# Attention with a window and sinks, then a gated two-layer product: w_out's rows dealt by four over the partitions, and half the masks of three units moved to TensorE

## The chip, the cores and the metric

The kernel runs on one core of a Trainium2 chip. Times are device microseconds of one execution; the median of three runs of the kernel before is 230.49 us (229.34 to 231.1). The profile is one execution more, which took 229.0 us; its span, from the first to the last instruction, is 227.2 us. The granted TensorE clock was 1.000 in it.

The engines are called PE (TensorE, matrix products), PEld (its loading of weights, the operand that stays in the array), ACT (ScalarE), DVE (VectorE), POOL (GpSimd) and SP (SyncE, which here only issues transfers). On TensorE the result is written to PSUM banks, from which ACT and DVE read.

## The reference

```python
def _attn_ref(q, k, v, n_sink, window):          # q, k, v: (4, 8, 768, 64)
    scores = (1 / sqrt(64)) * q @ k.T
    rel = pos[:, None] - pos[None, :]
    keep = (pos[None, :] < 4) | ((rel >= 0) & (rel < 128))
    a = softmax(where(keep, scores, -1e9))
    return a @ v

def _moe_ref(x, w_in, w_out, beta):              # (3072, 512), (512, 2048), (2048, 512), (2048,)
    h = x @ w_in
    g = h * (1 / (1 + exp(-beta * h)))
    return g @ w_out                             # (3072, 512), float32
```

The attention's output, turned to (token, head and dimension), is `x`. Each of the 2048 hidden columns has its own beta, and each is also one row of w_out; so the hidden columns may be taken in any order, as long as w_in's columns, beta and w_out's rows are taken in the same one.

## The kernel before

**Tiles.** The 3072 tokens are cut into T = 0 to 7 of 384 tokens. A unit n = 0 to 31 is one pair of heads over one such tile; units 4T to 4T+3 make tile T. A hidden block i = 16 T + m is 128 hidden columns (m = 0 to 15) of tile T.

**A unit** has these steps: its q and k come in as rows and are transposed so that the head dimension lies on the partitions (by TensorE and a copy for units 0 to 11, `transpose_first` and `transpose_in`; by a transposing transfer later); TensorE makes scores, ACT takes their exponential into E, a mask of zeros and ones is multiplied onto E by DVE, or was added to the scores as a large negative number by TensorE (units 0 to 3, `add_mask`, a product with the identity that opens the accumulation); `attend` multiplies E with v and a column of ones (line 843, with the sinks at line 832); `normalise` takes the reciprocal of the sums (852) and multiplies (854); `transpose_out` turns the result into xT, by TensorE and a copy for units 0 to 7, by a transposing transfer on SP's queue (863) later. Units 4 to 7 go by `scores_by_banks` (789) and `mask_by_banks` (804): scores and masks come in two banks, one of 512 columns per head and one of 256.

**A hidden block** is four products of 384 columns with w_in as weights (887), ACT's tanh with `beta_half` as its scale (895), and DVE's `g` (908), which is h (1 + tanh(beta h / 2)). **The output** is a sum over 16 hidden blocks (m) for each 128 tokens: products of 512 columns with `g` as weights (922), called products below, into two accumulators `acc0` and `acc1`, then a copy and a transfer out.

**Order.** The program runs over steps s. From s = 0 to 15 come the hidden blocks of T = 0; then a gap of eight steps (GAP = 8), in which units 4 to 7 run and only products stand beside them; then all other hidden blocks, with the units of the next tile between. `products(s)` says how many products step s names. A planner (class `Prog`) then lists the instructions of each engine: it keeps a cost for each, picks at each point the instruction that can start first by its costs, and models transfers by a rate, a start-up time per queue (`QUEUE`) and a `TAIL`. Every engine carries out its list in that order. Where the planner sees TensorE idle for more than `IDLE` = 50 ns ahead of a next step it puts in fillers (914), products of ones that nothing reads, for the idle time and `MORE` = 60 ns on top.

**Transfers.** SP's queue loads q, k and v of units 0 to 3, then waits for w_in's second quarter and loads those of units 4 to 7, then waits for parts of w_out for those of units 8 to 11 (535, 544). POOL issues w_in (596, four loads), w_out (601, eight loads of two m each) and the later units' rows (570, 579). beta comes in on ACT's queue as 16 rows of 128 and is transposed by TensorE (968) and halved by DVE (970).

The lines that the change touches: `Prog` (112 to 118), `load_qk` (537), `load_w_out` (600), `scores_by_banks`, `mask_by_banks`, `hidden_matmul` (887), beta (945, 968), and the main program.

Of the kernel before, what the change touches and what calls it, by code (L numbers as in the profile page):

```python
# [11 lines left out]
DM, DF, NOUT = 512, 2048, 512  # L12
NTOK = B * S
# [33 lines left out]
PE_MASK = 4  # L47

# [23 lines left out]
def products(s):  # L72

    return 0 if s < NM else 3 if s < NM + GAP or s >= 2 * NM + GAP else 2 if s < NM + GAP + 2 else 1
# [23 lines left out]
class Prog:  # L98
# [14 lines left out]
    TAIL, MIX, HEAVY, RING = 900.0, 1.1, 2.5, 8  # L113
# [4 lines left out]
    IDLE, MORE, EARLY = 50.0, 60.0, 5500.0  # L118
# [251 lines left out]
def bass_streamingllm_window__then__act_swish_beta_kernel(  # L370
# [32 lines left out]
    beta_stage = sb("beta_stage", (16, 128), F32)  # L403
# [5 lines left out]
    ident32 = sb("ident32", (32, 32), F32)  # L409
    scratch = sb("scratch", (32, 1), F32)  # L410
    mask = [sb(f"mask{z}", (128, 6, 128), BF16) for z in range(2)]
    add_mask = sb("add_mask", (128, 6, 128), BF16)
    stage = {t: [sb(f"{t}_stage{z}", (128, 2, 6, D), F32) for z in range(4)] for t in "qk"}
# [178 lines left out]
    w_out_src = moe_w_out.rearrange("(m p) n -> p m n", p=128)  # L592
# [176 lines left out]
    def scores_by_banks(n):  # L769
# [3 lines left out]
        for bank, runs in enumerate(AT_ONCE[half]):  # L773
            of = 2 - 2 * bank
            names = HS_NAMES[of:of + 2]
            src = hs_ps[:, of:of + 2, :]
            with P.together("pe"):
# [7 lines left out]
                for kb, qb, nq in runs:  # L785
                    w = 128 * nq
                    for hh in range(2):
                        rows = slice(64 * hh, 64 * hh + 64)
                        op("pe", lambda e, at=at, w=w, kb=kb, qb=qb, nq=nq, hh=hh, rows=rows, of=of: e.matmul(  # L789
                            hs_ps[:, of + hh, at:at + w], keys_of(pb, rows, kb),  # L790
                            queries_of(pb, rows, qb, nq), start=True, stop=True),
# [7 lines left out]
    def mask_by_banks(n):  # L799
        z, half = n % NE, place(n)[2]  # L800
        for bank, cols in enumerate((slice(0, 512), slice(512, 768))):
            m = mask[half][:, :, :].rearrange("p m x -> p (m x)")[:, cols]
# [3 lines left out]
               r=[("E", z, bank), *MASK[half]], w=[("E", z, bank)], **dve(580.0 if bank == 0 else 290.0))  # L806
# [77 lines left out]
    def hidden_matmul(i, c):  # L884
# [3 lines left out]
            bank, w_in16[:, c, m * 128:(m + 1) * 128], xT[:, c, T * TT:(T + 1) * TT],  # L888
# [31 lines left out]
    def project(T, t, m, bank, name, eng="act", cols=slice(0, NOUT), queue="sp"):  # L920
# [24 lines left out]
    op("act", lambda e: e.dma_start(beta_stage[:, :], moe_beta.rearrange("(m p) -> m p", p=128)),  # L945
       w=["beta_stage"], dma="beta", busy=500.0, lag=100.0)
# [85 lines left out]
    for s in range(-2, S_END + NM):  # L1032
# [114 lines left out]
```

## Time and profile before

| | us |
|---|---|
| median of three runs (lowest, highest) | 230.49 (229.34, 231.1) |
| the profiled execution | 229.0 |
| its span | 227.2 |
| first hidden product (line 887) | 17.07 |
| first hidden product of T = 1 | 42.99 |
| first hidden product of T = 2 | 70.39 |
| last product with w_out begins at about | 224.2 |

The page's costliest groups for TensorE, with the number of instructions, their busy time and the mean duration of one (matmuls overlap, so their starts are closer than the duration):

| line, what | count | busy us | mean ns |
|---|---|---|---|
| 887, hidden blocks | 480 | 96.2 | 326 |
| 922, products with w_out | 340 | 93.8 | 380 |
| 843, attend | 348 | 17.3 | 193 |
| 914, fillers | 32 | 6.7 | 344 |

A row of the engine timeline reads: start in us, duration, engine, line, operation, what is written from what, shape, how many are merged in the row, and in brackets how long the engine had been idle before and what it had waited for. In the chain of waits each row is a start, a length and what the time went to.

### The profile page before, as it was taken

The page shows a single profiled execution, that of the slowest core. Times are in us where ns is not written, and L with a number is a line of the kernel's source. Part 1 is how long each engine was busy: PE and PEld are TensorE (multiplying, and loading weights), DVE is VectorE, ACT ScalarE, POOL GpSimd, SP SyncE. Part 2 cuts the span into 40 slices and gives each one's busy share as a digit, 9 for nine tenths or more (in the row PEclk, how much of TensorE's full clock was granted, in tenths as well). Part 3 has the DMA queues.
Part 4 walks back from the last instruction along what each step waited for, and adds up shares of the span by engine and source line. Part 5 has one row for each costly group of instructions (what it writes and reads, how often), then busy time and mean ns, then how long its engine had stood idle before and what let it go on. Part 6 is the DMA issues. An engine that isn't in the chain of part 4 may idle for free.

```text
span 227.2 us, 4402 instructions
## 1 busy us (share of the span) xinstructions
PE 218.2 (96%) x1721; PEld 122.1 (54%) x1749; DVE 133.0 (59%) x263; ACT 141.7 (62%) x210; POOL 125.4 (55%) x193
## 2 busy tenths in 40 slices
PE   7999978899999999999999999999999999999995
PEld 4665545454655555555555555555555555555454
DVE  4756878459974666666565656555666564443200
ACT  3778796259855777666657676666656755555310
POOL 6692387999996969995939398876300000000000
PEclk9999999999999999999999999999999999999999
DMA  5999989999999989999979999999911112110122
GB/s 168 255 191 215 280 194 151 204 242 206 123 148 177 159 89 151 123 161 134 120 110 157 98 134 139 121 154 138 140 24 52 52 26 64 46 49 0 60 79 95
DMA packets 98389, 29.70 MB, mean 131 GB/s; under 512 B 84912, under 2 KB 95424, under 8 KB 98368
## 3 DMA queue, kind: packets, MB, share of 16 engines
q0 software_dynamic: 55888, 10.52, 58.2%
q1 hardware_dynamic: 42304, 18.75, 36.5%
q8 instruction: 14, 0.23, 0.4%
q10 hardware_dynamic: 176, 0.14, 0.2%
q14 instruction: 7, 0.06, 0.1%
HBM read 27.32 MB, written 6.29 MB: 148 GB/s over the span
## 4 chain that ended last, share of the span: by engine, by line
PE 73%; DMA 14%; SPq 6%; DVE 3%; issue 2%; POOL 1%; ACT 0%; ACTq 0%
PE hs_ps L887 31%; PE acc L922 30%; DMA k_stage<-in_k_dram 4%; PE hs_ps L754 4%; SPq L535 4%; PE hs_ps L843 3%; DMA q_stage<-in_q_dram 3%; DMA w_in<-in_moe_w_in_dram 3%; SPq L544 2%; DMA w_out<-in_moe_w_out_dram 2%; DMA xT<-o_norm 2%; PE hs_ps L922 2%; POOL qk L650 1%; PE hs_ps L832 1%; DVE g L908 1%
## 5 line engine op out<-in xcount | busy, mean ns | idle before, releaser
L895 ACT ACTIVATE th<-hs_ps,beta_half 128x384 f32<-128x384 f32 x120 | 69.3, 582 | 61.8 <-PE hs_ps L887 61.1
L887 PE MATMUL hs_ps<-xT,w_in 128*128 128x384 bf16 x480 | 96.2, 326 | 0.6 <-issue 0.2
L922 PE MATMUL acc<-w_out,g 128*128 128x512 bf16 x340 | 93.8, 380 | 1.3 <-issue 0.5
L908 DVE SCALAR_TENSOR_TENSOR g<-th,hs_ps 128x384 bf16<-128x384 f32 x120 | 65.5, 550 | 42.8 <-ACT th L895 41.3
L887 PEld LDWEIGHTS hs_ps<-xT,w_in 128*128 128x128 bf16 x480 | 45.6, 98 | 38.5 <-DVE g L908 1.2
L922 PEld LDWEIGHTS acc<-w_out,g 128*128 128x128 bf16 x368 | 33.6, 98 | 30.2 <-issue 3.8
L570 POOL DMA_DIRECT2D land<-in_q_dram x40 | 30.6, 767 | 15.9 <-DVE rden L852 15.9
L766 ACT ACTIVATE E<-hs_ps 128x1920 bf16<-128x1920 f32 (+1 forms) x20 | 32.8, 1640 | 0.3
L811 DVE TENSOR_TENSOR E<-E,mask 128x1536 bf16<-128x1536 bf16 x20 | 19.2, 959 | 21.2 <-ACT E L766 21.2
L570 POOL DMA_DIRECT2D land<-in_k_dram x40 | 30.6, 767 | 0.0
L579 POOL DMA_DIRECT2D v_aug<-in_v_dram x40 | 30.6, 767 | 0.0
L930 ACT ACTIVATE out_sb<-acc 128x512 f32<-128x512 f32 x23 | 13.7, 597 | 7.3 <-PE acc L922 7.1
L843 PE MATMUL hs_ps<-v_aug,E 128*128 128x65 bf16 x348 | 17.3, 193 | 0.1
L843 PEld LDWEIGHTS hs_ps<-v_aug,E 128*128 128x128 bf16 x348 | 15.7, 97 | 2.7 <-issue 1.3
L854 DVE TENSOR_TENSOR o_norm<-hs_ps,rden 128x384 bf16<-128x384 f32 x29 | 16.1, 556 | 1.0
L727 ACT ACTIVATE E<-hs_ps 128x768 bf16<-128x768 f32 x16 | 12.6, 814 | 1.9 <-PE hs_ps L720 1.7
L832 PE MATMUL hs_ps<-v_sink,E 128*128 128x130 bf16 x48 | 9.3, 219 | 1.1 <-DVE E L804 1.1
L754 PE MATMUL hs_ps<-qkT 64*128 64x256 bf16 (+2 forms) x144 | 10.1, 254 | 0.0
L795 ACT ACTIVATE E<-hs_ps 128x1024 bf16<-128x1024 f32 x8 | 7.8, 1038 | 2.2 <-PE hs_ps L789 2.2
L650 POOL CAST qk<-k_stage 128x384 bf16<-128x384 f32 x12 | 6.3, 526 | 4.8 <-DMA k_stage<-in_k_dram 4.5
L852 DVE RECIPROCAL rden<-hs_ps 128x6 f32<-128x6 f32 x29 | 5.6, 193 | 3.8 <-PE hs_ps L843 3.7
L914 PE MATMUL acc<-ones 128*128 128x384 bf16 (+1 forms) x32 | 6.7, 344 | 1.2 <-DVE ones L457 1.2
(73 smaller groups left out, 148.1 us busy)
## 6 DMA issues: line engine op xcount, KB each, us to landing
out_dram<-out_sb SPq DMA_DIRECT2D x23, 256.0 KB, 2.7
q_stage<-in_q_dram SPq DMA_DIRECT2D x12, 192.0 KB, 6.4
k_stage<-in_k_dram SPq DMA_DIRECT2D x12, 192.0 KB, 6.2
w_in<-in_moe_w_in_dram POOLq DMA_DIRECT2D x4, 512.0 KB, 6.5
w_out<-in_moe_w_out_dram POOLq DMA_DIRECT2D x8, 256.0 KB, 5.9
land<-in_q_dram POOLq DMA_DIRECT2D x40, 48.0 KB, 3.7
land<-in_k_dram POOLq DMA_DIRECT2D x40, 48.0 KB, 3.6
v_aug<-in_v_dram POOLq DMA_DIRECT2D x40, 48.0 KB, 3.5
```

Of the source, the lines that this page charges most:

```text
L570: op("gp", lambda e, d=d, s=s: e.dma_start(d, s), w=[("land", pb, half, x, hh)], after=after, dma=f"l{pb}{half}{x}{hh}", **transfer(TT * D ...
L579: op("gp", lambda e, d=d, s=s: e.dma_start(d, s), w=[("v", pb, 3 * half + c, hh) for c in range(3)], after=after, dma=f"lv{pb}{half}{hh}", ...
L754: op("pe", lambda e, at=at, w=w, kb=kb, qb=qb, nq=nq, hh=hh, rows=rows, bank=bank: e.matmul(hs_ps[:, of + 2 * hh + bank, at:at + w], keys_ ...
L766: op("act", lambda e: e.activation(dst, src, AF.Exp, bias=0.0, scale=SCALE), x=list(names), w=[("E", z, 0), ("E", z, 1)], **act(1920 if ha ...
L811: op("dve", lambda e: e.tensor_tensor(E[z][:, :, 0:768], E[z][:, :, 0:768], m.unsqueeze(1).to_broadcast([128, 2, 768]), ALU.mult), r=[("E" ...
L843: last=(x == len(kbs) - 1): e.matmul(av_ps[:, at + hh * D1:at + hh * D1 + D1], E[z][:, hh, col:col + 128], v_aug[:, pb, hh, kb, 0:D1], sta ...
L854: op("dve", lambda e: e.tensor_tensor(o_norm[o][:, :, :, :].rearrange("p m h d -> p (m h) d"), src[:, :, 0:D], rden[z][:, :].unsqueeze(2). ...
L887: op("pe", lambda e: e.matmul(bank, w_in16[:, c, m * 128:(m + 1) * 128], xT[:, c, T * TT:(T + 1) * TT], start=(c == 0), stop=(c == 3)), r= ...
L895: op("act", lambda e: e.activation(th[i % 3][:, :], bank, AF.Tanh, bias=0.0, scale=beta_half[:, m:m + 1]), x=[name], r=["beta"], w=[("th", ...
L908: op("dve", lambda e: e.scalar_tensor_tensor(g[T % 2][:, m, :], th[i % 3][:, :], 1.0, bank, ALU.add, ALU.mult), r=[("th", i % 3)], x=[name ...
L922: op("pe", lambda e: e.matmul(bank[:, 0:width], g[T % 2][:, m, t * 128:(t + 1) * 128], w_out16[:, m, cols], start=(m == 0), stop=(m == NM ...
L930: op("act", lambda e: e.activation(out_sb[z][:, 0:width], bank[:, 0:width], AF.Copy, bias=0.0, scale=0.5), x=[name], w=[("out_sb", z)], ** ...
```

## The change

Four things are changed together.

1. Rows of w_out. Before, w_out's row m * 128 + p lay on partition p as block m. Now 512 rows at a time are dealt by four (`PER`): partition p holds rows 512 g + 4 p + j, j = 0 to 3, as blocks 4 g + j. A load of two blocks takes two neighbouring rows per partition as one piece of 4 KB (two pieces of 2 KB before). The hidden blocks take the same columns: the weights of block m are every fourth column of w_in from m % 4, within 512. beta is loaded straight into that order, by SP after the first loads of v, as 512 pieces of four numbers; ACT's load, its transpose on TensorE and the small identity for it are gone.
2. Masks. For the bank of 512 columns of units 5, 6 and 7 the mask is added by TensorE: a product of the identity with `add_mask1` (0 or -1e6) opens each head's accumulation, and DVE's multiplication for that bank is left out. `add_mask1` is made from the mask by one POOL instruction ahead of the first w_out load.
3. Products in the gap: steps 16 to 19 name none, steps 20 to 23 six each (three in each of the eight steps before).
4. The planner's numbers: `TAIL` 1100 (900), `MORE` 0 (60), DVE's mask costs 700 and 330 (580 and 290), w_out's rate 385 (350), and unit 8's q load counted 2300 ns late. Unit 7's copy of transposed q and k goes to DVE (ACT before).

The transfers, the products and the order that is planned change so:

```diff
+PE_MASK_BANKS = ((5, 0), (6, 0), (7, 0))
...
 def products(s):
 
+    if NM <= s < NM + GAP:
+        return (0,0,0,0,6,6,6,6)[s - NM]
...
-    TAIL, MIX, HEAVY, RING = 900.0, 1.1, 2.5, 8
+    TAIL, MIX, HEAVY, RING = 1100.0, 1.1, 2.5, 8
...
-    IDLE, MORE, EARLY = 50.0, 60.0, 5500.0
+    IDLE, MORE, EARLY = 50.0, 0.0, 5500.0
...
-           dma=f"{name}{pb}_{half}", seq="loads " + queue, late=3300.0 if (n, x) == (4, 0) else 0.0,
+           dma=f"{name}{pb}_{half}", seq="loads " + queue, late=3300.0 if (n, x) == (4, 0) else 2300.0 if (n, x) == (8, 0) else 0.0,
...
-    w_out_src = moe_w_out.rearrange("(m p) n -> p m n", p=128)
+    w_out_src = moe_w_out.rearrange("(g p j) n -> p g j n", p=128, j=PER)
...
-        op("gp", lambda e: e.dma_start(w_out16[:, m:m + ms, :], w_out_src[:, m:m + ms, :]), after=after,
+        op("gp", lambda e: e.dma_start(w_out16[:, m:m + ms, :].rearrange("p j n -> p (j n)"),
+                                         w_out_src[:, m // PER, m % PER:m % PER + ms, :].rearrange("p j n -> p (j n)")), after=after,
            w=[("w_out", mm) for mm in range(m, m + ms)],
-           dma=f"wo{m}", **transfer(ms * 128 * NOUT * 4, 350, 740.0, 3.0))
+           dma=f"wo{m}", **transfer(ms * 128 * NOUT * 4, 410 if ms == 4 else 385, 740.0, 3.0))
...
+            masked = (n, bank) in PE_MASK_BANKS
+            if masked:
+                cols = slice(0, 512) if bank == 0 else slice(512, 768)
+                with P.together("pe"):
+                    for x in range(2):
+                        op("pe", lambda e, x=x, of=of, cols=cols: e.matmul(
+                            hs_ps[:, of + x, 0:cols.stop - cols.start], ident[:, :], add_mask1[:, cols],
+                            start=True, stop=False, skip_group_check=True),
+                           r=["ident", "add_mask1"], w=[names[x]], **pe(cols.stop - cols.start))
...
         for bank, cols in enumerate((slice(0, 512), slice(512, 768))):
+            if (n, bank) in PE_MASK_BANKS:
+                continue
...
-               r=[("E", z, bank), *MASK[half]], w=[("E", z, bank)], **dve(580.0 if bank == 0 else 290.0))
+               r=[("E", z, bank), *MASK[half]], w=[("E", z, bank)], **dve(700.0 if bank == 0 else 330.0))
...
-            bank, w_in16[:, c, m * 128:(m + 1) * 128], xT[:, c, T * TT:(T + 1) * TT],
+            bank, w_in16[:, c, m // PER * 512 + m % PER:m // PER * 512 + 512:PER], xT[:, c, T * TT:(T + 1) * TT],
...
-    op("act", lambda e: e.dma_start(beta_stage[:, :], moe_beta.rearrange("(m p) -> m p", p=128)),
-       w=["beta_stage"], dma="beta", busy=500.0, lag=100.0)
...
+    op("sp", lambda e: e.dma_start(beta_raw[:, :].rearrange("p (g j) -> p g j", j=PER),
+                                   moe_beta.rearrange("(g p j) -> p g j", p=128, j=PER)),
+       w=["beta_raw"], dma="beta", seq="loads sp", busy=500.0, lag=300.0)
+    op("dve", lambda e: e.tensor_scalar(beta_half[:, :], beta_raw[:, :], 0.5, None, ALU.mult),
+       r=["beta_raw"], w=["beta"], **dve(100.0))
...
-    select(ident32[:, :], ones32[:, :], [[1, 32]], ALU.is_equal, 0.0, 0, -1, ["ones32"], ["ident32"])
     transpose_first(0)
-    op("pe", lambda e: nc.tensor.transpose(acc[1][:, 0:16], beta_stage[:, :], ident32[0:16, 0:16]),
-       r=["beta_stage", "ident32"], w=["acc1"], **pe(64))
-    op("dve", lambda e: e.tensor_scalar(beta_half[:, :], acc[1][:, 0:16], 0.5, None, ALU.mult),
-       x=["acc1"], w=["beta"], **dve(100.0))
...
+    op("gp", lambda e: e.tensor_scalar(
+        add_mask1[:, :], mask[1][:, :, :].rearrange("p m x -> p (m x)"), -1.0, -NEG, ALU.add, ALU.mult),
+       r=MASK[1], w=["add_mask1"], busy=1000.0, lag=140.0, after=[("v", 3, 0, 0)])
...
-                transpose_in(n, eng="act" if n in (5, 7) else "dve")
+                transpose_in(n, eng="act" if n in (5,) else "dve")
```

More of the change, by code (lines that the diff above doesn't have):

```diff
@@ L12 @@
 DM, DF, NOUT = 512, 2048, 512
+PER = 4
 NTOK = B * S
@@ L402, in bass_streamingllm_window__then__act_swish_beta_kernel @@
     w_out16 = sb("w_out16", (128, NM, NOUT), BF16)
-    beta_stage = sb("beta_stage", (16, 128), F32)
+    beta_raw = sb("beta_raw", (128, NM), F32)
     beta_half = sb("beta_half", (128, NM), F32)
@@ L408, in bass_streamingllm_window__then__act_swish_beta_kernel @@
     ones32 = sb("ones32", (32, 32), F32)
-    ident32 = sb("ident32", (32, 32), F32)
     scratch = sb("scratch", (32, 1), F32)
@@ L412, in bass_streamingllm_window__then__act_swish_beta_kernel @@
     add_mask = sb("add_mask", (128, 6, 128), BF16)
+    add_mask1 = sb("add_mask1", (128, 6 * 128), BF16)
     stage = {t: [sb(f"{t}_stage{z}", (128, 2, 6, D), F32) for z in range(4)] for t in "qk"}
@@ L788, in scores_by_banks @@
                         rows = slice(64 * hh, 64 * hh + 64)
-                        op("pe", lambda e, at=at, w=w, kb=kb, qb=qb, nq=nq, hh=hh, rows=rows, of=of: e.matmul(
+                        op("pe", lambda e, at=at, w=w, kb=kb, qb=qb, nq=nq, hh=hh, rows=rows, of=of, masked=masked: e.matmul(
                             hs_ps[:, of + hh, at:at + w], keys_of(pb, rows, kb),
-                            queries_of(pb, rows, qb, nq), start=True, stop=True),
+                            queries_of(pb, rows, qb, nq), start=not masked, stop=True,
+                            skip_group_check=masked),
                            r=keys_read(pb, half, runs), w=[names[hh]],
```

## The prediction

> **What bounds the kernel now.** First the page's busy times, then busy time by stage: T=0's attention (to 17.07 us), its hidden blocks (to 28.9), units 4 to 7 (to 43), T=1's hidden blocks (to 66.8), the rest.
>
> ```profile
> span 227.2 us, 4402 instructions
> PE 218.2 (96%) x1721; PEld 122.1 (54%) x1749; DVE 133.0 (59%) x263; ACT 141.7 (62%) x210; POOL 125.4 (55%) x193
> ```
> ```profile
> 17.07:28.90 11.83, 11.62 (x83) 6.89 (x80) 8.94 (x17) 9.73 (x20) 3.17 (x8) 1.00 1.20 250
> 28.90:43.00 14.10, 12.16 (x144) 6.86 (x146) 10.75 (x23) 9.36 (x11) 12.17 (x20) 1.00 0.99 171
> 43.00:66.80 23.80, 22.64 (x193) 12.10 (x194) 18.81 (x38) 15.73 (x26) 22.60 (x33) 1.00 1.62 187
> 90.90:150.00 59.10, 58.67 (x461) 32.44 (x468) 35.89 (x68) 38.65 (x55) 46.58 (x63) 1.00 1.23 132
> ```
> Columns: the stretch, its length, then busy PE, weight loads, DVE, ACT, POOL, granted clock, DMA share, GB/s. TensorE is the bound: from 90.9 to 150 it is idle for 0.4 us. Its idle time lies early: 1.94 us in units 4 to 7 (14.10 - 12.16), 1.16 in T=1's hidden blocks. A change that leaves the hidden blocks and products alone is worth that idle time plus what it moves ahead of 17.07, minus what it adds to PE. The PE timeline says what the largest idle pieces wait for:
>
> ```profile
> 33.26 0.23 PE L832 MATMUL hs_ps<-v_sink,E 128*128 128x130 bf16 x1 [0.76 <-DVE E L804]
> ...
> 35.82 0.23 PE L832 MATMUL hs_ps<-v_sink,E 128*128 128x130 bf16 x1 [0.32 <-DVE E L804]
> ...
> 45.48 0.34 PE L663 MATMUL hs_ps<-ident,qk 128*128 128x128 bf16 x3 [0.82 <-POOL qk L650]
> ```
> Two are waits for VectorE's mask, one for unit 8's cast, whose load waited for w_out: in the chain of waits w_out's landing (32.86 + 4.50) is followed by unit 8's q load (37.38 + 7.48) and this cast (44.92).
>
> **Masks on TensorE.** Removed from DVE: three masks of 128x1024, 0.68 us each (2.05). Added to PE: six matmuls of 512 columns; products of that width stand 0.216 us apart (three in 0.65), so 1.29 us. Unit 7's q/k copy goes from ACT (0.79) to DVE (0.94). Hidden in idle time the six cost nothing, and all 1.94 us filled would leave -0.65; on the path they cost +1.29. I replayed the new order by the rows' durations. Unit 5's pair (0.43) falls into the 0.76 that PE waits for unit 4's mask. That mask stays on DVE, and one of the 128x512 forms took 1.33 us where the shortest took 0.42, so unit 4's attend remains at about 33.3. Unit 6's pair follows that attend; unit 5's attend, relieved of its large mask, moves from 35.82 to about 35.5. Then what is late is unit 7's copy, now in DVE's queue ahead of unit 5's normalisation: the transposes out of unit 4 wait for its bank until about 36.4. The products held back for units 6 and 7 fill PE afterwards. T=1's first hidden block comes out at 42.9 (42.99 before), with 20 products done in both orders. I take 0.0, ends -0.65 and +1.29. The additive mask is built on POOL: 768 columns at the cast's 0.51 per 384, about 1.0 us, between 17.5 and the first w_out load at 18.11. It delays that load by 0.4; the load landed at 25.9 and its first product ran at 29.99: free. One new filler of 128 columns: +0.05.
>
> **w_out dealt.** Same bytes, eight loads of 0.716 us on POOL, half the pieces. The landings were 3.5 to 8.7 us; nothing waited on w_out but SP's loads of units 8 to 11 (8.4 us in three waits), and of these PE feels the 0.82 at 45.48. The new order also puts unit 8's q transposes after the third hidden block instead of the first, some 2 us later, so that idle goes with or without faster pieces: -0.82, at least 0.
>
> The price is in w_in: each hidden weight load now takes every fourth column, 8 bytes apart. No row shows that. The nearest are these:
>
> ```profile
> 12.51 0.55 PE L843 MATMUL acc<-v_aug,E 128*128 128x65 bf16 x12
> 12.89 0.32 PE L709 MATMUL hs_ps<-add_mask,ident 128*128 128x384 bf16 x1
> ```
> Twelve matmuls, each with its own load of 128 contiguous columns, took 12.89 - 12.51 = 0.38 us, 32 ns for a load and its matmul, although each load's record is 98 ns. A hidden block's matmul of 384 columns occupies PE for 162.5 ns (four in 0.65). Even at four times 32 ns, for four times the span of bytes, a strided load takes 127 ns and stays behind the matmul before it: 0. The other end, twice the 98 ns record with no overlap within it, is 196 ns: 512 x 33.5 = +17.2 us. A gain is excluded, since the loads are hidden already. The Trainium skill ("SBUF — State Buffer", in the section "Door 1") says that reads in the same 16-byte line run at full bandwidth if at least two fall in it. By it a step of 8 bytes costs nothing and the sum is the same; no run here shows it yet.
>
> **Beta.** Gone are ACT's issue (0.43), a POOL select (about 0.22) and a PE transpose at 3.30, while q and k of unit 0 were still on their way: 0. New is a load of 512 pieces of 16 bytes at the end of SP's first loads, and DVE's beta copy (0.17), which waits for it. Behind that copy in DVE's queue stands unit 1's reciprocal (13.09 before); for it wait accumulator 1, unit 2's attend and, through PE's order, the first hidden block. Nearest rows: the v loads issued just ahead on the same queue have 512 pieces each as well (of 256 bytes), were issued at 7.15 to 8.21 and landed 4.0 us later. The next issue is at 8.75, when SP has nothing to do until 17.84, where unit 4's loads wait for w_in, so its 0.5 of issue is free: landing at 12.75, copy done at 12.9, no wait. Ends: 2.1 us, beta's landing before; 7.9, the slowest v load, which lands it at 16.65 and moves the reciprocal by 3.7. I take 4.0. The pieces also cost the DMA engines 512 x 31.4 ns / 16 = 1.0 us (31.4 = 36.5% of 227.2 x 16 over 42304 packets), while w_in lands; its chunks have 1.4 us or more in hand (23.9 against 25.33 for the last), but unit 4's loads, which wait for the second, come up to 1.0 later and its k transposes stand only 0.65 later in the new order: 0 to +0.4, I take +0.2. The Trainium skill ("DMA: Bandwidth & Descriptors", Specifications) speaks against this edit: pieces below 512 bytes cost a read-modify-write. The v loads at 256 bytes lie below that line too, and landed in 4.0 us.
>
> **Fillers and order ahead of 17.07.** With 60 ns less per gap, seven fillers of 128 columns fewer run there. A filler of 0.22 us after unit 0's attend goes and unit 2's first scores move ahead of unit 3's k transposes: its exponential can start at 11.64 (11.91), unit 3's ends at 14.75 (15.2), the first hidden block starts at 16.65: -0.4. Unit 4's data don't come earlier, so I count -0.2, ends -0.4 and 0.
>
> **Into T=2.** PE now has 66 products done when it reaches T=2, 59 before, and unit 11's attend comes later. From its end to the fourth matmul of T=2, which reads unit 11's transposed output, stand 19 products (4.1), unit 12's scores (0.7) and three matmuls (0.5): 5.3 us. Before, the attend ended near 64.6, the normalisation at 65.78, and this row followed:
>
> ```profile
> 66.78 4.30 DMA xT<-o_norm
> ```
> That is 1.2 + 4.3 = 5.5 us without a queue, 1.0 more behind SP's transpose of unit 14, which stands ahead there in the new order too. PE waited 0.47 for it before. Change: -0.47 to +1.3; I take +0.2.
>
> **Sum.** 0.0 + 0.05 - 0.82 + 0 + 0.2 - 0.2 + 0.2 = -0.57, some -0.6: span 226.6, that execution 228.4 instead of 229.0 (1.8 around the span). The median of the three runs is 230.49, 1.5 above the profiled one; on it 229.9.
>
> **Rivals.** (1) PE's idle time goes altogether: -0.65 in units 4 to 7, -1.16 in T=1, -0.47 into T=2, -0.4 ahead of 17.07: -2.7, 227.8. For it: PE holds back products that can fill any gap, and DVE is relieved by 2.05 us. Against it: the wait for unit 4's mask stays, and the loads of unit 4 don't come earlier. Chance 0.32.
> (2) Beta lands late and DVE stands on it. At 7.9 us after issue the first hidden block starts some 3.5 later in place of 0.2 earlier, in all +3.1: 233.6. It decides from a landing 4.3 us after issue, and exceeds 1% from about 7. For: 512 tiny pieces in a saturated stage (DMA share 1.2). Against: the v rows. 0.12.
> (3) Strided weight loads come out from behind the matmuls, from 162.5 ns a load; at 196 ns +17.2 - 0.6: 247. Against: 32 ns a pair. 0.08.
> (4) Unit 11's output is the new wait into T=2, +1.3 instead of +0.2: 231.0. 0.08.
> (5) The change doesn't do what it says: w_out's landings stay and the 0.82 only moves to unit 8's or 9's later transposes: 230.7. 0.05.
>
> **Numbers.** Forecast 0.35. One per cent is 2.3 us and about what a measurement of this kernel can tell from no change. Faster by more: rival 1, 0.32. Within: 0.35 + 0.08 + 0.05 = 0.48. Slower: 0.12 + 0.08 = 0.20. Range 227.3 to 232.6: from just below rival 1 past rival 4 and the unfilled masks (229.9 + 1.29 = 231.2) into rival 2; rival 3 and the late end of rival 2 are left out.
>
> **What would show it.** Hidden matmuls still 0.65 us for four (else rival 3). DVE's beta copy starting before 13 and the first hidden block before 17.07 (else rival 2). Idle time of PE between 28.9 and 43 near 0.7, with a wait for unit 4's mask left, and T=1 starting near 42.9. No wait for unit 8's cast. A wait for unit 11's output below 0.7 us. The forecast is wrong if T=1's first hidden block moves by over 1 us, or if hidden blocks change their pace.

## The result, and the profile after

The kernel after takes 231.06 us (median of 14 runs, 229.53 to 233.5); the kernel before, run beside it, 229.93 (14 runs). The ratio is 1.0052, with a 95% interval of 1.0028 to 1.0077: slower by 1.2 us, within the one per cent that I called "same", but on the slower side of no change, where the forecast was on the faster. A ratio compares the faster executions of a kernel with those of before made beside it and leaves out the slower ones, so it need not be the quotient of the two medians. The profiled execution of after took 231.4 us, 2.4 more than that of before, so it shows the loss about twice as large as the runs do; single traces are read below for what waits on what, and the runs for what it is worth.

The page of after, its busy times:

```profile
span 229.7 us, 4436 instructions
PE 220.7 (96%) x1755; PEld 129.6 (56%) x1755; DVE 132.3 (58%) x261; ACT 141.8 (62%) x209; POOL 124.8 (54%) x193
```

Busy time by stage, in the stretches of the prediction (stretch, its length, busy PE, weight loads, DVE, ACT, POOL, clock, DMA share, GB/s):

```profile
17.07:28.90 11.83, 11.20 (x78) 7.39 (x77) 8.06 (x15) 9.21 (x19) 3.90 (x9) 1.00 1.13 226
28.90:43.00 14.10, 12.97 (x152) 7.27 (x151) 10.25 (x22) 9.62 (x11) 8.94 (x17) 1.00 0.87 154
43.00:66.80 23.80, 23.32 (x182) 12.90 (x181) 17.59 (x35) 15.03 (x24) 22.84 (x33) 1.00 1.60 204
90.90:150.00 59.10, 59.10 (x476) 35.04 (x475) 37.35 (x71) 40.24 (x57) 49.30 (x66) 1.00 1.29 133
```

TensorE is still the bound, with no idle time at all from 90.9 to 150. Where units 4 to 7 run it is idle for 1.13 us (1.94 before), DVE is busy for 0.5 us less, and the DMA engines moved 154 GB/s in place of 171. The trace of before needs care here: it has no record for 28 of the 368 products with w_out, though their weight loads are there. All of its 0.43 us of idle time from 90.9 to 150 stand at such products, and 0.37 of the 1.94. So 1.13 compares with about 1.6. The PE timeline says what it waits for now:

```profile
26.71 0.34 PE L669 MATMUL hs_ps<-ident,qk 128*128 128x128 bf16 x3 [0.46 <-POOL qk L656]
...
42.60 1.04 PE L940 MATMUL acc<-w_out,g 128*128 128x512 bf16 x4 [0.60 <-DMA w_out<-in_moe_w_out_dram]
...
44.06 0.39 PE L940 MATMUL acc<-w_out,g 128*128 128x512 bf16 x1 [0.42 <-DMA w_out<-in_moe_w_out_dram]
...
74.56 0.35 PE L905 MATMUL hs_ps<-xT,w_in 128*128 128x384 bf16 x1 [1.39 <-DMA xT<-o_norm]
```

Of the three waits of before, the two for VectorE's masks are gone (0.18 us for unit 5's second bank is left) and so is the one for unit 8's cast. Two new ones stand in their place: the products wait 1.02 us for w_out itself, which nothing on TensorE did before, and the fourth matmul of T = 2 waits 1.39 us for unit 11's output. (Before, TensorE had no idle time there: the weight load waited 0.47 us, and the matmul came 0.25 us behind its pace. In after the weight load waits 1.76, and the matmul comes 1.55 behind.) The first hidden block starts at 17.25 us (17.07), T = 1's at 45.10 (42.99), T = 2's at 72.52 with 66 products done (70.39 with 59).

How far one trace can be trusted shows in a kernel below that differs from before only in the stride of its weights and has a ratio of 1.0015: in its trace T = 1 starts at 44.36 and T = 2 at 72.54, both over 1 us later than in the trace of before. The trace of before is an early one of its order.

How late w_out lands is read from the tile's own view: the last four loads, and the time from issue to landing. Of before:

```profile
L601 POOL DMA_DIRECT2D w_out<-in_moe_w_out_dram x4: 716/716/716, 35.4 to 37.6; - x4
...
DMA to landing us min/median/max: 5.6/7.0/8.7
```

Of after:

```profile
L606 POOL DMA_DIRECT2D w_out<-in_moe_w_out_dram x4: 528/542/558, 36.5 to 38.1; - x4
...
DMA to landing us min/median/max: 7.5/8.9/10.5
```

POOL issues a load in 0.54 us in place of 0.72, and the three figures for the four loads are 1.8 to 1.9 us longer. So half the pieces didn't make the load faster.

### The profile page after: what moved, and what is told of

The parts are those of the page before. It is cut to its first block, busy times and chain, and to the rows that moved or that the text cites. A ratio compares the mean times of both kernels' runs of the same rounds, so it can differ in the third digit from the quotient of the medians.

```text
span 229.7 us, 4436 instructions
## 1 busy us (share of the span) xinstructions
PE 220.7 (96%) x1755; PEld 129.6 (56%) x1755; DVE 132.3 (58%) x261; ACT 141.8 (62%) x209; POOL 124.8 (54%) x193
## 3 DMA queue, kind: packets, MB, share of 16 engines
HBM read 27.32 MB, written 6.29 MB: 146 GB/s over the span
## 4 chain that ended last, share of the span: by engine, by line
PE 75%; DMA 7%; POOL 5%; issue 5%; DVE 3%; SPq 2%; ACT 2%; POOLq 0%; ACTq 0%
PE acc L940 31%; PE hs_ps L905 31%; PE hs_ps L760 4%; DMA w_out<-in_moe_w_out_dram 3%; PE hs_ps L861 3%; DMA xT<-o_norm 2%; SPq L540 2%; DMA k_stage<-in_k_dram 2%; PE hs_ps L940 2%; POOL qk L656 1%; DVE g L926 1%; ACT th L913 1%; DVE o_norm L872 1%; POOL v_aug L554 1%; PE hs_ps L850 1%
## 5 line engine op out<-in xcount | busy, mean ns | idle before, releaser
L940 PE MATMUL acc<-w_out,g 128*128 128x512 bf16 x368 | 99.2, 380 | 1.0 <-DMA w_out<-in_moe_w_out_dram 1.0
L905 PEld LDWEIGHTS hs_ps<-xT,w_in 128*128 128x128 bf16 x480 | 53.1, 114 | 33.4 <-DMA xT<-o_norm 1.8
L656 POOL CAST qk<-q_stage 128x384 bf16<-128x384 f32 x8 | 4.1, 509 | 7.5 <-DMA q_stage<-in_q_dram 7.4
```

Source lines behind the costliest of these rows:

```text
L905: op("pe", lambda e: e.matmul(bank, w_in16[:, c, m // PER * 512 + m % PER:m // PER * 512 + 512:PER], xT[:, c, T * TT:(T + 1) * TT], start= ...
L940: op("pe", lambda e: e.matmul(bank[:, 0:width], g[T % 2][:, m, t * 128:(t + 1) * 128], w_out16[:, m, cols], start=(m == 0), stop=(m == NM ...
```

## The experiments

My theories at the start were: A, the dealt transfers are late (4-KB pieces of w_out, 512 small pieces of beta); B, the new order of products and the masks; C, the weights at a stride. A table of all runs stands at the end of the section.

**Taking the dealing out.** The first kernel is after in its exact order, with w_out and w_in's columns undealt; the second has the planner plan anew without the dealing.

```diff
-    w_out_src = moe_w_out.rearrange("(g p j) n -> p g j n", p=128, j=PER)
+    w_out_src = moe_w_out.rearrange("(m p) n -> p m n", p=128)
...
-            bank, w_in16[:, c, m // PER * 512 + m % PER:m // PER * 512 + 512:PER], xT[:, c, T * TT:(T + 1) * TT],
+            bank, w_in16[:, c, m * 128:(m + 1) * 128], xT[:, c, T * TT:(T + 1) * TT],
```

> The changed kernel with the order of every engine kept, but w_out's rows and w_in's columns as before (pieces of 2 KB, weights of contiguous columns); beta keeps its new load and so stands in another order than the columns. Theory A (late transfers: w_out lands later in pieces of 4 KB, and beta's 512 pieces push w_in): PE's waits for w_out (0.60 and 0.42 us in the changed kernel) go, the fifth and later w_out loads land within 8.7 us of their issue, ratio to before 1.000 to 1.003. Theory B (the new order and the masks on PE cost it): 1.005 as the changed kernel. Theory C (strided weight loads cost it): 1.000 or below, with hidden blocks closer together than in the changed kernel.

Ratio 1.0016 (0.9981 to 1.0051): 0.36 per cent below after, but the intervals overlap.

> The changed kernel without the dealing: w_out, w_in's columns and beta as in the kernel before (beta by ACT and a transpose), with the masks on PE, the order of products and the planner's numbers as changed. Theory A: 0.996 to 1.000. Theory B: 1.004 to 1.007. Theory C: 0.996 to 1.000, so that it needs the strided kernel beside it.

Ratio 0.9984 (0.9956 to 1.0012): without the dealing, and with beta's old load, the loss is gone. T = 2's wait for unit 11's output is still there (1.26 us), so it belongs to the masks and the order.

**The weights at a stride, alone**, on the kernel before:

```diff
-            bank, w_in16[:, c, m * 128:(m + 1) * 128], xT[:, c, T * TT:(T + 1) * TT],
+            bank, w_in16[:, c, m // 4 * 512 + m % 4:m // 4 * 512 + 512:4], xT[:, c, T * TT:(T + 1) * TT],
```

> The kernel before with one edit: the hidden blocks take every fourth column of w_in as weights, while w_out's rows and beta stay, so that the sum pairs other columns than the reference. Theory A and B: weight loads of 114 ns instead of 98, four hidden matmuls still 0.65 us apart, ratio 0.999 to 1.001. Theory C: 1.004 or more.

Ratio 1.0015 (0.9982 to 1.0049). The page's group of weight loads of after, against 98 ns before, and its matmuls:

```profile
L905 PE MATMUL hs_ps<-xT,w_in 128*128 128x384 bf16 x480 | 95.5, 326 | 1.4 <-DMA xT<-o_norm 1.4
...
L905 PEld LDWEIGHTS hs_ps<-xT,w_in 128*128 128x128 bf16 x480 | 53.1, 114 | 33.4 <-DMA xT<-o_norm 1.8
```

Each load is 16 ns longer and each matmul of 326 ns as before: the load is hidden. No loss is seen from the stride, and the 1.004 or more of theory C lies above all but the end of the interval.

**beta.** First in after, beta as four rows of 2 KB into a tile that nothing reads; then the new load alone on the kernel before; then after with beta loaded early by ACT and turned by four small transposes.

```diff
-    op("sp", lambda e: e.dma_start(beta_raw[:, :].rearrange("p (g j) -> p g j", j=PER),
-                                   moe_beta.rearrange("(g p j) -> p g j", p=128, j=PER)),
+    fill("dve", beta_raw[:, :], 1.0, ["beta_ones"])
+    op("sp", lambda e: e.dma_start(beta_stage[:, :], moe_beta.rearrange("(m p) -> m p", p=512)),
```

> The changed kernel with one edit: beta's load is 4 pieces of 2 KB into a tile that nothing uses, at the same place in SP's queue, and DVE's copy waits for it and halves ones, so tanh's scale is 0.5 instead of beta / 2. Theory A: w_in's second load lands near 17.9 instead of 18.9, unit 4's q is cast near 25 instead of 26.16, PE's wait of 0.46 for it goes, ratio to before 1.001 to 1.003. Theories B and C: 1.005 as the changed kernel.

Ratio 1.0092 (1.0052 to 1.0132): not faster, against theory A's beta part. Why it is slower than after is not shown.

```diff
-    op("act", lambda e: e.dma_start(beta_stage[:, :], moe_beta.rearrange("(m p) -> m p", p=128)),
...
+    op("sp", lambda e: e.dma_start(beta_raw[:, :].rearrange("p (g j) -> p g j", j=4),
+                                   moe_beta.rearrange("(g p j) -> p g j", p=128, j=4)),
```

> The kernel before with beta taken as in the kernel after: SP issues the load of 512 sixteen-byte pieces ahead of unit 2's q, DVE halves it; ACT's early load, the 32x32 identity and PE's transpose of beta are gone. (beta's columns then belong to dealt rows while the hidden rows are undealt; the amount of work is the same.) Theory A: SP is one issue of 0.6 us later from there on, v's and w_in's transfers land 0.3 to 1 us later, the first hidden matmul comes 0.2 to 0.6 us later than 17.07, and the time is 0.1 to 0.4 per cent longer (230.0 to 230.7 us). Theories B and C: within 0.15 per cent of before. The rival inside A, that the pieces of w_out alone make the loss: no difference here and the whole 0.5 to 0.7 per cent in the run with w_out's pieces alone.

Ratio 1.0027 (0.9996 to 1.0059): +0.6 us, not clear of nothing.

```diff
-    op("sp", lambda e: e.dma_start(beta_raw[:, :].rearrange("p (g j) -> p g j", j=PER),
+    op("act", lambda e: e.dma_start(beta_stage[:, :], moe_beta.rearrange("(m p) -> m p", p=512)),
...
+        for j in range(PER):
+            op("pe", lambda e, j=j: nc.tensor.transpose(acc[1][:, 4 * j:4 * j + 4], beta_stage[:, j::PER], ident32[0:4, 0:4]),
```

> The kernel after with beta loaded early by ACT in four rows of 2 KB and turned by four small PE transposes (as before, four instead of one), so SP's extra load and the 512 small pieces are gone; all else is after's. If beta's load is the loss (the beta part of theory A): the first hidden matmul falls back to about 17.0 us, SP's later issues are 0.6 us earlier, and the ratio to before falls from 1.0052 to about 1.000 to 1.002. If the pieces of w_out are the loss: first hidden as in before, yet the products still wait 0.4 to 1 us for w_out near 42 to 45 us and the ratio stays at 1.004 to 1.006. Theories B and C: 1.005.

Ratio 1.005 (1.0005 to 1.0095), as after. So no part of the loss is seen to be beta's. Yet the load of 512 pieces is not free. It landed 3.8 us after issue in the trace of after, but 5.0 to 5.9 in four other traces that hold it. In one of them DVE stood on it for 2.09 us (row of the DVE timeline, after with 2-KB pieces, a kernel below):

```profile
14.55 0.17 DVE L979 TENSOR_SCALAR beta_half<-beta_raw 128x16 f32<-128x16 f32 x1 [2.09 <-DMA beta_raw<-in_moe_beta_dram]
```

Its first hidden block started at 18.28 us. In after with the stores on ACT (also below) DVE stood on it for 1.93 us, and the first hidden block started at 18.49. In the kernel before with this load, planned anew, DVE's wait was 0.92 us and the first hidden block started at 17.17.

**w_out's loads alone**, on the kernel before with its order unaltered on every engine:

```diff
-    w_out_src = moe_w_out.rearrange("(m p) n -> p m n", p=128)
+    w_out_src = moe_w_out.rearrange("(g p j) n -> p g j n", p=128, j=4)
```

> The kernel before with one thing altered: w_out's rows are dealt in its load, so that each of the eight two-row pieces is read as 4 KB in a row on a partition; the order on every engine is that of before, instruction for instruction. (The hidden rows stay undealt, so the products pair other rows of w_out with them; the amount of work is the same.) Theory A (the larger pieces land later and hold up the products of T=0): the last piece lands about 2 us later than the 46.3 us of before, POOL issues a piece in 0.54 us instead of 0.72, products wait for w_out between 42 and 46 us, and the time is 0.2 to 0.6 per cent longer (230.2 to 231.2 us beside 229.8). Theories B and C: within 0.15 per cent of before.

Ratio 1.0108 (1.0056 to 1.0159), in six runs: this one part makes a loss of its own. That it is larger than the whole change's is not borne out by its neighbours below, at 1.003 to 1.0065. Then which of the eight loads, with sixteen bytes left free in SBUF between two rows where a load was to take 2-KB pieces:

> The kernel before, order on every engine unaltered, with w_out's rows dealt and only the first of its eight loads (issued at 18 us, beside the q, k and v of units 4 to 7) in 4-KB pieces; the other seven have sixteen bytes between the rows and so 2-KB pieces. (Products pair dealt rows with undealt hidden rows; the amount of work is the same.) With all eight at 4 KB the ratio was 1.0108. If the loss comes from the loads of units 4 to 7 that run beside the first piece: 1.005 to 1.010 here and the casts of units 4 and 5 come about 1 us later than in before. If it comes from the seven pieces and the loads of units 8 to 11 behind them: within 0.2 per cent of before.

> The converse: the first load of w_out in 2-KB pieces, the other seven in 4-KB pieces, order that of before, rows dealt (same amount of work). If the seven pieces make the loss: 1.005 to 1.010, the wait for unit 8's cast near 45 us 1 to 2 us in place of 0.82, since SP's loads of units 8 to 11 are issued behind those pieces. If the first piece makes it: within 0.2 per cent of before. If each makes half: both kernels at 1.003 to 1.006.

Ratios 1.0065 (1.0028 to 1.0102) and 1.0032 (0.9986 to 1.0078). The first is clear of 1 and the second is not. The size of the pieces was the wrong thing to ask about, as the next run shows.

**The size of the pieces, in after itself.** Everything of the change stays, but each row of a pair is its own 2-KB piece again:

```diff
+        at, step = w_out_at[m], w_out_at[m + 1] - w_out_at[m]
+        return w_out16[:, at:at + ms * step].rearrange("p (j n) -> p j n", j=ms)[:, :, 0:NOUT]
...
+        op("gp", lambda e: e.dma_start(w_out_rows(m, ms), w_out_src[:, m // PER, m % PER:m % PER + ms, :]), after=after,
```

> The kernel after with sixteen bytes left free between the two rows of each pair of w_out in SBUF, so that a load can't take both rows as one piece: 2 KB a piece as before, POOL's issue 0.72 us again; the order on every engine is that of after, instruction for instruction, and all else of the change stays. Theory A, now narrowed to w_out's 4-KB pieces: the loss goes, ratio 0.996 to 1.001 (about that of the change without dealing, 0.9984). Theory B (the order and the masks) and C (weights at a stride) and beta's load: the ratio stays at 1.004 to 1.006.

Ratio 1.0063 (1.0027 to 1.0098), all of the loss with 2-KB pieces, and the last four loads land as late as in after:

```profile
L612 POOL DMA_DIRECT2D w_out<-in_moe_w_out_dram x4: 713/727/741, 37.0 to 39.1; - x4
...
DMA to landing us min/median/max: 7.1/9.0/10.7
```

So theory A was right about w_out and wrong about why. What is left of the dealing is which addresses a load reads: undealt, a load of two blocks reads 256 rows that follow one another in DRAM; dealt by fours, it reads two rows, leaves out two, reads two, over a stretch of 1 MB.

**Size against addresses.** On before's order, dealt addresses with 2-KB pieces (padding as above), and 4-KB pieces without gaps (rows dealt in twos, so that a load's pieces follow one another):

```diff
-    w_out_src = moe_w_out.rearrange("(m p) n -> p m n", p=128)
+    w_out_src = moe_w_out.rearrange("(g p j) n -> p g j n", p=128, j=2)
```

> The kernel before, order on every engine unaltered, with w_out's rows dealt (a load takes two neighbouring rows out of every four, so its reads lie 8 KB apart) but sixteen bytes left between the two rows in SBUF, so that each piece is 2 KB as in before. (Products pair dealt rows with undealt hidden rows; the amount of work is the same.) With 4-KB pieces the same kernel was at 1.0108. If the addresses that the dealing reads cost the time (theory A2): 1.004 to 1.010. If the size of the pieces does (theory A1): within 0.25 per cent of before. If neither, and the ratios of 1.003 to 1.011 of the dealt kernels are spread of their own: anything up to 1.003, the two kernels of this pair alike.

> The kernel before, order on every engine unaltered, with w_out's rows dealt in twos (rows 2p and 2p+1 of 256 on partition p), so that each load takes 4-KB pieces as in the run with w_out's pieces alone, but its pieces follow one another in DRAM without a gap. (Products pair other rows with the hidden rows; same amount of work.) Theory A1, the size: 1.004 to 1.010. Theory A2, the gaps of 4 KB between the reads: within 0.25 per cent of before.

1.0053 (1.0007 to 1.0099) with gaps; 1.0031 (0.9976 to 1.0086) without, too wide to decide. The same edit in after decides it. (The weights then lie at a stride of two columns in place of four, and their loads' median falls from 113 to 98 ns; the run with the stride alone shows no time for that.)

> The kernel after, order on every engine unaltered, with w_out's rows dealt in twos in place of fours: 4-KB pieces still, but each load's pieces follow one another in DRAM, where after's lie 8 KB apart with 4 KB left out between them; weights of the hidden matmuls at a stride of two columns to match. (beta's load is after's, so its columns belong to the dealing in fours; the amount of work is the same.) In the traces so far the four last pieces of w_out land 5.1 to 5.9, 6.0 to 7.4, 7.4 to 8.0 and 8.5 to 9.3 us after issue in the nine kernels whose loads have no gaps, whether 2 or 4 KB, and 6.4 to 7.5, 7.2 to 9.4, 8.4 to 10.4 and 9.4 to 11.5 us in the nine with gaps. Theory A2 (the gaps): the four pieces land as in the first group here, and the ratio falls from 1.0052 to 0.998 to 1.002. If the gaps only move the landings and the loss is elsewhere: landings of the first group with a ratio of 1.004 to 1.007.

Ratio 0.9961 (0.9912 to 1.001), below the interval of after: closing the gaps takes the loss away, with the order, the masks, the 4-KB pieces and the beta load as they were. Its size is less sure: the medians of all executions, 231.31 beside 231.11 of before, stand at 1.0009, where after's stood at 1.0049. With 2-KB pieces in the same order the pair points the same way, 1.0063 with gaps and 1.0016 undealt. PE's idle wait for w_out is gone in its trace. The landings moved only half as far as I had expected:

```profile
L606 POOL DMA_DIRECT2D w_out<-in_moe_w_out_dram x4: 528/542/558, 37.2 to 38.7; - x4
...
DMA to landing us min/median/max: 6.5/7.8/9.4
```

**The wait into T = 2.** The masks alone on before, dealing, products and planner's numbers left out:

```diff
+PE_MASK_BANKS = ((5, 0), (6, 0), (7, 0))
...
-                transpose_in(n, eng="act" if n in (5, 7) else "dve")
+                transpose_in(n, eng="act" if n in (5,) else "dve")
```

> The kernel before with the masks of the first bank of units 5 to 7 on PE and nothing else of the change: no dealing, beta as before, products ahead of units 4 to 7 not held back, the planner's numbers those of before. Theory B (the masks and the order are worth little, and the order makes T=2's wait for xT): without the held-back products the wait for w_out near 42 us goes below 0.2 us, and the time is 0.2 to 0.5 per cent shorter than before (228.7 to 229.4 us) if the masks pay for themselves, or within 0.15 per cent if the six matmuls of 512 columns only trade their 0.22 us each for DVE's 0.6 us. If T=2's wait of 1.3 us is there too without the held-back products, the masks and not the order of products made it.

Ratio 1.0033 (0.9996 to 1.007), and T = 2 waits 1.85 us: the masks bring this wait by themselves, without the held-back products. To take the wait away, T = 0's three stores go from SP's queue to ACT's, in the change without dealing, in after, and in before:

```diff
-                project(T, t, m, acc[a][:, :], f"acc{a}")
+                project(T, t, m, acc[a][:, :], f"acc{a}", queue="act" if T == 0 else "sp")
```

> The change without dealing, with the three stores of T=0's outputs issued by ACT in place of SP (in SP's queue one of them stood directly ahead of the transpose of unit 11's output that T=2 waits for). The transposes that followed such a store landed 5.3 to 6.4 us after issue, those without one 4.0 to 4.6. If the place in SP's queue makes the wait: the wait into T=2 falls from 1.26 to under 0.5 us and the ratio from 0.9984 to 0.994 to 0.997. If it is the store's traffic, whoever issues it, or unit 11's later place on PE: the wait stays above 1 us and the ratio is 0.997 to 1.000.

Ratio 0.9899 (0.984 to 0.9958), six runs; no wait into T = 2. Once more:

> The kernel without dealing and with T=0's stores issued by ACT once more, unaltered: its ratio of 0.9899 came from six runs, the least of any. Added to after the same edit took the ratio from 1.0052 to 0.9995, and added to before it gave 1.002. If the two parts add up (no dealing 0.9984, the stores some 0.5 per cent): 0.992 to 0.996. If the six runs were lucky: 0.996 to 0.999.

Ratio 0.9906 (0.9872 to 0.994): 229.2 us beside 231.11 of before, faster than before, and by the ratios faster than after.

> The kernel after with T=0's three stores issued by ACT in place of SP, as in the run that did so without dealing (0.9899). If the order around T=2 is a loss of its own in after (the wait of 1.39 us for unit 11's output, and the products that the planner moves into the room), the ratio falls by 0.5 to 0.9 per cent, from 1.0052 to 0.996 to 1.000, with no wait above 0.5 us into T=2. If the gain of that run was spread of its six runs, the ratio stays at 1.003 to 1.006.

> The kernel before with T=0's three stores issued by ACT in place of SP, nothing else. Before's wait for xT into T=2 is 0.47 us in its trace, so at most that can be had: 0.998 to 1.001. If the stores on ACT are worth 0.5 per cent or more by themselves, without the masks on PE (another order of the products, not that wait): 0.990 to 0.995.

0.9995 (0.9955 to 1.0035) in after, 1.002 (0.998 to 1.006) in before: worth something only where that wait is. (Without dealing the ratio falls by 0.8 per cent, 1.8 us, while the wait in the trace falls by 1.1. The intervals allow that, and no run says more.) How it works is not what I expected. The chain of waits of after into T = 2, then of the second run of the version without dealing:

```profile
68.20 0.56 DVE o_norm L872
69.14 5.38 DMA xT<-o_norm
```
```profile
67.25 0.56 DVE o_norm L872
67.83 5.37 DMA xT<-o_norm
```

The transpose lands 5.4 us after its issue in both, so the store ahead of it in SP's queue did not slow it. Over all traces the long landing goes with the masks: 5.25 to 6.29 us in nine kernels with masks on TensorE, wherever the stores are issued, and 3.96 to 4.90 in eight without. What slows it is not shown. In the second run it is issued 0.4 us sooner after the normalisation, and the planner, which no longer sees the store on SP, puts 21 products and unit 12's attend (0.55) between unit 11's attend and T = 2's first block, where after has 19 products. The same landing is hidden by more work (PE timeline, version without dealing):

```profile
68.83 3.19 PE L940 MATMUL acc<-w_out,g 128*128 128x512 bf16 x14
...
73.25 0.99 PE L905 MATMUL hs_ps<-xT,w_in 128*128 128x384 bf16 x5 [0.19 <-DMA xT<-o_norm]
```

**All together.** "Gaps" says whether w_out's loads leave out rows; the last columns are PE's idle time for w_out and for unit 11's output, in one trace each (a dash: no trace that compares with the others).

| order | gaps | piece | ratio (95%) | w_out us | T = 2 us |
|---|---|---|---|---|---|
| before | no | 2 KB | 1 | 0 | 0 |
| before, weights at a stride | no | 2 KB | 1.0015 (0.9982 to 1.0049) | 0 | 0 |
| before | no | 4 KB | 1.0031 (0.9976 to 1.0086) | 0 | 0 |
| before | yes | 2 KB | 1.0053 (1.0007 to 1.0099) | 0.3 | 0.4 |
| before | yes | 4 KB | 1.0108 (1.0056 to 1.0159) | 0 | 0 |
| before | yes | first 4, rest 2 KB | 1.0065 (1.0028 to 1.0102) | 0.8 | 0 |
| before | yes | first 2, rest 4 KB | 1.0032 (0.9986 to 1.0078) | - | - |
| before, new load of beta | no | 2 KB | 1.0027 (0.9996 to 1.0059) | 1.2 | 0.4 |
| before, stores on ACT | no | 2 KB | 1.002 (0.998 to 1.006) | 0 | 0.2 |
| before, masks on TensorE | no | 2 KB | 1.0033 (0.9996 to 1.007) | 0 | 1.9 |
| after, undealt | no | 2 KB | 1.0016 (0.9981 to 1.0051) | - | - |
| change planned without dealing | no | 2 KB | 0.9984 (0.9956 to 1.0012) | 0.5 | 1.3 |
| the same, stores on ACT, first time | no | 2 KB | 0.9899 (0.984 to 0.9958) | 1.3 | 0 |
| the same, stores on ACT, once more | no | 2 KB | 0.9906 (0.9872 to 0.994) | 0.6 | 0.2 |
| after, dealt in twos | no | 4 KB | 0.9961 (0.9912 to 1.001) | 0 | 1.7 |
| after | yes | 4 KB | 1.0052 (1.0028 to 1.0077) | 1.0 | 1.4 |
| after, 2-KB pieces | yes | 2 KB | 1.0063 (1.0027 to 1.0098) | 1.7 | 1.3 |
| after, beta as rows that nothing reads | yes | 4 KB | 1.0092 (1.0052 to 1.0132) | 1.3 | 2.3 |
| after, beta by TensorE | yes | 4 KB | 1.005 (1.0005 to 1.0095) | - | - |
| after, stores on ACT | yes | 4 KB | 0.9995 (0.9955 to 1.0035) | 1.8 | 0.6 |

From the issue of the fifth load to the landing of the last it took 10.6 to 11.4 us (mean 11.0) in ten traces without gaps and 11.4 to 13.1 (mean 12.2) in seven with them. That is where the traces show the gaps; how they reach the end differs by order. In after and the kernels made from it the products wait for w_out: 1.0 to 1.8 us with gaps, 0 to 1.3 without. In the kernel before with the new load of beta they wait 1.2 us without gaps, so such a wait is not the gaps' alone. In before's order SP issues the loads of units 8 to 11 behind it; but PE's wait for unit 8's cast, 0.82 us in before's trace, is 1.7 to 2.3 in six of seven others of that order, with gaps and without, so there the way is not shown.

## Why the prediction was wrong

**The step that failed is "w_out dealt"**, with its price "-0.82, at least 0". I reasoned from bytes and pieces: the same bytes, half the pieces, so no slower. The addresses changed too, and no term of the sum stood for that. Measured, the dealing costs 0.68% (0.9984 to 1.0052), 1.6 us, if the kernel planned without it is the measure (beta's load goes with it there), and closing its gaps alone gives 0.9% back; the other figures for it lie between 0.4 and 0.9%. The cast's wait did go, as argued, by the new order (and 0.82 was a small measure of it: 1.7 to 2.3 us in six other traces of before's order); but in that order the products in the gap come to stand on w_out, which I had as waited for by SP alone.

**Into T = 2**: forecast +0.2, and rival 4 at +1.3, 0.08. The 0.47 that I took for PE's wait was the weight load's; the like figure of after is 1.76, so the trace has +1.3, and the runs give 0.6% in after (1.0052 to 0.9995) and 0.8% without dealing (0.9984 to 0.9906) when it is covered. Rival 4 was there. The count of work in between was right (5.3 us); the row that I set against it, a landing of 4.30, became 5.38, and lies above 5.2 in every trace with the masks on TensorE that is compared above. Why it does is open.

**Masks on TensorE**: forecast 0.0. Both waits for VectorE's mask went, also the one for unit 4's that I expected to stay. The idle time that I set out to fill was smaller than I read it, 1.57 us without the products that have no record. Masks, product order and planner's numbers without the dealing and with T = 2's wait covered are at 0.9906, -2.2 us; my terms for them (masks 0.0, filler +0.05, cast -0.82, order -0.2) made -0.97. So the sum erred on both sides: a gain of 2.2 taken as 1.0, and two losses of 1.6 and 1.3 to 1.8 taken as 0 and 0.2. The gain and the losses come from the same ratios, so that they add up proves nothing by itself. Rival 1, that all idle time goes, is near in time for the version without dealing and with the stores on ACT (its 227.8 is 1.2% below 230.49, and 0.9906 is 0.9), though that version still waits 0.6 us for w_out; after itself gave the gain back at two places.

**Beta**: forecast +0.2, landing 4.0 us after issue. In after's trace it landed after 3.8; in four others after 5.0 to 5.9, beyond the 4.3 us from which rival 2 decides. So the wait of rival 2 happens in some executions, and moved the first hidden block by over 1 us in two of them. Its price in time is +0.6 us (-0.1 to +1.4, the load alone in before), which is not clear of nothing, and not +3.1.

**Weights at a stride**: 0, right. Matmuls keep 0.65 us for four; the median load grew from 98 to 113 ns, under the 127 that I had allowed. The Trainium skill ("SBUF — State Buffer", Specifications) has reads run at full bandwidth with two hits per 16-byte line; the row differs by those 15 ns, though nothing of them reaches the time.

**Order ahead of 17.07**: forecast -0.2. The first hidden block came at 17.25 in after and at 17.19 to 17.22 in the three traces of the planned version without dealing: no gain.

**The signs I named.** The pace of the hidden blocks held; DVE's copy started before 13 in after, but the first hidden block at 17.25, not before 17.07; no wait for unit 8's cast. Idle time from 28.9 to 43 was 1.13 in place of 0.7, T = 1 started at 45.10 in place of 42.9 (the 1 us by which I called the forecast wrong), and the wait for unit 11's output was above 0.7. Those three point at the two places that the runs then showed, though a single trace of before's order without gaps also starts T = 1 at 44.4.

## What to carry to other kernels

A load that is rearranged so that its pieces grow may still read DRAM with gaps; price the addresses of one load, not only its bytes and pieces, and keep what one load reads in one stretch. When a wait goes away, ask what the freed order now stands on: here products came to wait for a load that only a queue had waited for, and a tile's first block for a transpose. A part that gains and a part that loses can hide each other in one change; running the parts apart found, with one further edit, a version 0.9% faster than before in a change that was 0.5% slower. And one trace is one execution: look at a second trace of the same order before pricing a wait from it, and count an engine's records before calling a stretch idle.

## What the hardware showed that I had not expected

**Gaps.** With 4 KB left out between reads of 4 KB, or between pairs of 2 KB, the last four loads of w_out came through 1.2 us later on the mean (12.2 against 11.0; the two ranges touch at 11.4). Why (banks, channels, or the other reads of the same stretch at the same time) is not shown. The Trainium skill ("DMA: Bandwidth & Descriptors", "Latency and other measured facts") gives copies between tensors in HBM a rate that falls with the row pitch, 207 GB/s at 512 KiB and 164 at 2 MiB; the pitch here is 8 KB, for which it has no figure.

**A small copy held up.** DVE's copy of 128x16 took 0.17 to 0.28 us in three traces with the new load of beta, 0.56 in a fourth, and in after:

```profile
12.71 1.06 DVE L974 TENSOR_SCALAR beta_half<-beta_raw 128x16 f32<-128x16 f32 x1
13.62 0.18 DVE L870 RECIPROCAL rden<-acc 128x6 f32<-128x6 f32 x1
```

POOL had a cast from 12.81 to 13.34 and a transfer's issue to 13.77. The Trainium skill ("SBUF — State Buffer", "Who interferes with whom") says that an instruction such as this one can enter a mode of DVE that takes a port shared with GpSimd, and that one of the two engines then waits for the other's whole instruction. The traces here do not settle it: in after with 2-KB pieces the copy took 0.17 us in the middle of POOL's issue of w_in (14.38 to 15.88), and in after dealt in twos 0.28 beside a cast (14.21 to 14.73). What held the copy stays open.

**Weight loads by stride.** 98 ns with columns side by side, 98 with every second (4 bytes), 113 with every fourth (8 bytes).
